# Filter loads regrouped over two queues, half of an angle table on GpSimd and a small identity made earlier, in a fused Fourier-filter and gated-MLP kernel

## The chip, the cores and the metric

The kernel runs on one core of one Trainium2 chip. The metric is the time of one execution on the device, in microseconds (us), lower is better. Before the change: 802.13 us (median of 3 runs, 801.12 to 802.29).

Names of engines in the profile: PE is TensorE's matmuls, PEld its weight loads, DVE is VectorE, ACT ScalarE, POOL GpSimd, SP SyncE. A "q" behind an engine's name is its sequencer, which issues DMA transfers.

## The reference

```python
# x: [8, 3008, 256], filt_r and filt_i: [1505, 256]
X = np.fft.rfft(x, axis=1)
y = np.fft.irfft(X * (filt_r + 1j * filt_i)[None], n=3008, axis=1)
# then, on the 24064 tokens, w_in: [256, 2048], w_out: [2048, 256], beta: [2048]
h = y.reshape(24064, 256) @ w_in
out = (h * sigmoid(beta * h)) @ w_out
```

## The kernel before

The Fourier transforms are matmuls: 3008 = 47 x 64, first a transform of length 47, then one of length 64 with the twiddle factors in its table (`t2`), then the product with the filter, then the same two steps backwards. The tables are made on the core, from angles and the sine function. Seven of the eight batches are filtered in the shadow of the MLP, whose 752 steps (`hps`, `gT`, `acc`) keep PE busy. The first batch can't hide: everything it needs must be done before the first MLP matmul. I call the time up to that matmul **the head**.

```python
KG = 6                                   # the 24 rows of the filter come in groups 0-5, 6-11, 12-23
x_cur = load_x(0, X_FIRST)               # six loads on GpSimd's queue (they cast to bf16)
bt = ...; nc.sync.dma_start(bt[:], moe_beta...)

mark = dpool.tile([1, D], BF16, name="mark", tag="mark")
nc.sync.dma_start(mark[:], x_cur[:1, JG, :])      # a tiny store: SyncE stands here until the
                                                  # third load of x has landed
...
FG = ((0, KG), (KG, KG), (2 * KG, 2 * KG))
for k0, n in FG:
    load_filter(fr_sb, filt_r, 0, k0, n, nc.sync) # real half: partitions 0-63 of fr_sb (two loads)
for k0, n in FG:
    load_filter(fr_sb, filt_i, M, k0, n, gp)      # imaginary half: partitions 64-127, GpSimd's queue
WG = NFB // 4
ws = [load_wout(i * WG, WG) for i in range(2)]    # SyncE's queue
...                                               # GpSimd: `keep`, five tiny operations
held = setup.tile([P, 1], F32, name="held", tag="held")
for p0 in (H, M + H):                             # GpSimd stands here until group 1 has landed,
    gp.tensor_copy(held[p0 : p0 + H], fr_sb[p0 : p0 + H, 2 * KG - 1, :1])
for h in range(WI):
    gp.dma_start(win_sb[:, :, fs], ...)           # then loads w_in, and later x of the second batch
# ... tables, angles(0, nc.vector), angles(1, nc.vector), first1(0..7) = first stage, 8 x 8 matmuls ...

def beta_columns():                               # in the loop below, at i == 3
    bps = hpsum.tile([P, NFB], F32, name="bps", tag="hps")
    id_f = setup.tile([NFB, NFB], F32, name="id_f", tag="id_f")
    gp.tensor_copy(id_f[:], ident[:NFB, :NFB])
    nc.tensor.transpose(bps[:], bt[:], id_f[:])
    ...

def product(i):                                   # 12 of them, for two rows each
    ...                                           # 4 matmuls into ps and ps2q
    for dst, ps in zip((p_t, q_t), pss):
        nc.vector.tensor_tensor(dst[:], ps[:], fr_sb[:, 2 * i : 2 * i + 2, :], ALU.mult)

for i in range(NK // 2 + FLAG):
    product(i); ...; t2_part(1, i); ...           # t2_part(1, .): ScalarE, needs angles(1)
    if i == 3: t2_more(1, nc.vector); beta_columns()
    ...
```

In the MLP's first steps the kernel loads both filter halves once more, in another layout (`uf`: `fi_sb` at step 1, the real half a few steps later, 3 MB), and the second batch's first-stage result goes through memory to be turned (`d<-a` writes it, `a<-d` reads it). The second batch's next stage, at step 22, needs all of these.

Of the kernel before, what the change touches and what calls it, by code (L numbers as in the profile page):

```python
# [9 lines left out]
P = 128  # L10
# [3 lines left out]
F32 = mybir.dt.float32  # L14
# [10 lines left out]
M = 64  # L25
H = M // 2
NK = 24
J = 32
KG = 6
NG = NK // KG  # L30
JG = 8
# [5 lines left out]
def kernel(  # L37
# [10 lines left out]
    nc = tc.nc  # L48

    B, S, D = x.shape  # L50
    NF = filt_r.shape[0]
    DIN, FF = moe_w_in.shape
# [4 lines left out]
    NFB = FF // P  # L57
# [8 lines left out]
    dpool = ctx.enter_context(tc.tile_pool(name="dram_scratch", bufs=2, space=bass.MemoryType.DRAM))  # L66
# [18 lines left out]
    fr_sb = consts.tile([P, NK, D], F32, name="fr_sb", tag="fr_sb")  # L85
# [8 lines left out]
    ident = consts.tile([P, P], BF16, name="ident", tag="ident")  # L94
# [3 lines left out]
    win_sb = wpool.tile([P, NDC, FF], BF16, name="win_sb", tag="win_sb")  # L98
# [4 lines left out]
    def evac(dst, src, on_act, scale=None):  # L103
        if on_act:
            nc.scalar.activation(dst, src, ACT.Copy, scale=1.0 if scale is None else scale)  # L105
        elif scale is None:
            nc.vector.tensor_copy(dst, src)  # L107
        else:
            nc.vector.tensor_scalar_mul(dst, src, scale)  # L109

    def load_x(b, parts):
        t = xpool.tile([NP, J, D], BF16, name="xg", tag="xg")
        xv = x[b].rearrange("(p j) d -> p j d", j=J)
        for p0, p1, j0, j1 in parts:
            nc.gpsimd.dma_start(t[p0:p1, j0:j1, :], xv[p0:p1, j0:j1, :])  # L115
        return t
# [7 lines left out]
    def load_filter(f_sb, filt, at, k0, n, eng, later=False):  # L124
        lo = AP(filt.tensor, filt.offset + k0 * D, [[N1 * D, H], [1, n * D]])
        hi = AP(filt.tensor, filt.offset + (N1 - k0) * D, [[N1 * D, H], [-D, n], [1, D]])
        units = [
            lambda: eng.dma_start(
                f_sb[at : at + H, k0 : k0 + n, :].rearrange("p k d -> p (k d)"), lo
            ),  # L130
            lambda: eng.dma_start(f_sb[at + H : at + M, k0 : k0 + n, :], hi),
        ]
        if later:
            return units
        for go in units:
            go()

    def load_wout(f0, n):
        ws = ostp.tile([P, n, D], F32, name="ws", tag="ost")
        nc.sync.dma_start(  # L140
            ws[:], moe_w_out[f0 * P : (f0 + n) * P, :].rearrange("(fb fp) j -> fp fb j", fp=P)
        )
        return ws

    def scale_wout(ws, f0, n, eng):
        for i in range(n):
            eng.tensor_scalar_mul(
                wout_sb[:, f0 + i, :], ws[:, i, :], rbeta_sb[:, f0 + i : f0 + i + 1]
            )
# [3 lines left out]
    setup = sp.enter_context(tc.tile_pool(name="setup", bufs=1))  # L153
# [25 lines left out]
    def warm(n, cols=512):  # L179
        for _ in range(n):  # L180
            nc.tensor.matmul(pw[0][:, :cols], lhsT=wz[:, :P], rhs=wz[:, :cols], start=True, stop=True)
# [5 lines left out]
    x_cur = load_x(0, X_FIRST)  # L187
# [1 line left out]
    nc.sync.dma_start(bt[:], moe_beta.rearrange("(fb fp) -> fb fp", fp=P))  # L189

    mark = dpool.tile([1, D], BF16, name="mark", tag="mark")
    nc.sync.dma_start(mark[:], x_cur[:1, JG, :])

    gp = nc.gpsimd
    ip_f = small("ip_f")
# [3 lines left out]


    FG = ((0, KG), (KG, KG), (2 * KG, 2 * KG))
    for k0, n in FG:
        load_filter(fr_sb, filt_r, 0, k0, n, nc.sync)
    for k0, n in FG:
        load_filter(fr_sb, filt_i, M, k0, n, gp)

    WG = NFB // 4
    ws = [load_wout(i * WG, WG) for i in range(2)]

    m_p = small("m_p")  # L210
    gp.tensor_scalar(m_p[:], ip_f[:], float(M), float(-M), ALU.is_ge, ALU.mult)
# [2 lines left out]
    gp.tensor_tensor(keep[:], keep[:], m_p[:], ALU.mult)  # L214
    gp.tensor_scalar(keep[:], keep[:], 0.5, None, ALU.is_gt)


    held = setup.tile([P, 1], F32, name="held", tag="held")
    for p0 in (H, M + H):
        gp.tensor_copy(held[p0 : p0 + H], fr_sb[p0 : p0 + H, 2 * KG - 1, :1])  # L220
    WI = 2
    for h in range(WI):
        fs = slice(h * FF // WI, (h + 1) * FF // WI)
        gp.dma_start(win_sb[:, :, fs], moe_w_in[:, fs].rearrange("(dc p) f -> p dc f", p=P))

    pre = small("pre")
    nc.scalar.activation(pre[:], wz[:, :1], ACT.Silu)
# [42 lines left out]
    def angles(h, eng):  # L270
        u = setup.tile([P, NH, M], F32, name="u", tag=f"u{h}")
        r = setup.tile([P, NH, M], F32, name="r", tag=f"r{h}")
        eng.tensor_tensor(
            u[:],
            ka[:, h * NH : (h + 1) * NH].unsqueeze(2).broadcast_to([P, NH, M]),
            kb[:].unsqueeze(1).broadcast_to([P, NH, M]),
            ALU.add,
        )
        eng.tensor_scalar(r[:], u[:], ROUND_C, ROUND_C, ALU.add, ALU.subtract)
        eng.tensor_tensor(u[:], u[:], r[:], ALU.subtract)  # L280
        us.append(u)
        rs.append(r)

    def t2_part(h, part):
        u, r = us[h], rs[h]
        ks_ = slice(h * NH, (h + 1) * NH)
        if part == 0:
            nc.scalar.activation(t2[:, ks_, 2, :], u[:], ACT.Sin, scale=TWO_PI)
        elif part == 1:
            nc.scalar.activation(r[:], u[:], ACT.Abs)  # L290
        else:
            for cols, sgn, b in ((slice(0, H), -1.0, hp), (slice(H, M), 1.0, hm)):
                nc.scalar.activation(
                    t2[:, ks_, 1, cols], r[:, :, cols], ACT.Sin, scale=sgn * TWO_PI, bias=b[:]
                )
# [5 lines left out]
        eng.tensor_copy(t2[:, ks_, 0, :], t2[:, ks_, 1, :])  # L301

    angles(0, nc.vector)
    angles(1, nc.vector)


    a_t = ypool.tile([P, NDC, NK, J, 4], BF16, name="a_t", tag="y")
# [1 line left out]
    def first1(i, on_act):  # L309
        for dc in range(NDC):  # L310
            if dc:
                ps = opsum.tile([P, 4, P], F32, name="psa", tag="acc")
            else:
                ps = fpsum.tile([P, 4, P], F32, name="psa", tag="f")
            for e in range(4):
                nc.tensor.matmul(
                    ps[:, e, :KP],
                    lhsT=x_cur[:, 4 * i + e, dc * P : (dc + 1) * P],
                    rhs=t1b[:],
                    start=True,  # L320
                    stop=True,
                )
            evac(
                a_t[:, dc, :, 4 * i : 4 * i + 4, :].rearrange("p k j a -> p j k a"),
                ps[:, :, :KP].rearrange("p j (k a) -> p j k a", a=4),
                on_act[dc],
            )
# [2 lines left out]
        first1(i, (True, True))  # L330
        warm(2)
    t2_part(0, 0)
    first1(2, (True, True))
    warm(2)
    for part in (1, 2):
        t2_part(0, part)
# [5 lines left out]
    warm(2)  # L342
    first1(6, (True, True))
    warm(2)
    first1(7, (False, True))

    xs = {}
    if B > 1:
# [42 lines left out]

    def beta_columns():
        bps = hpsum.tile([P, NFB], F32, name="bps", tag="hps")
        id_f = setup.tile([NFB, NFB], F32, name="id_f", tag="id_f")
        gp.tensor_copy(id_f[:], ident[:NFB, :NFB])
        nc.tensor.transpose(bps[:], bt[:], id_f[:])
        tiny = setup.tile([P, NFB], F32, name="tiny", tag="tiny")
        nc.vector.tensor_copy(beta_sb[:], bps[:])
        gp.tensor_tensor(tiny[:], beta_sb[:], beta_sb[:], ALU.mult)
        gp.tensor_scalar(tiny[:], tiny[:], 1e-12, 2e-6, ALU.is_lt, ALU.mult)  # L400
        gp.tensor_tensor(beta_sb[:], beta_sb[:], tiny[:], ALU.add)
        gp.tensor_copy(
            t1.rearrange("p (a k) -> p a k", a=4), t1b.rearrange("p (k a) -> p a k", a=4)
        )
# [56 lines left out]
    for i in range(NK // 2 + FLAG):  # L461
        if i < NK // 2:
            product(i)
        if i % 3 < 2 and i // 3 < 3:
            turn_a(2 + 2 * (i // 3) + i % 3, True)
        if i < 3:
            t2_part(1, i)
        if i % 3 > 0 and i // 3 < 3:
            table3(1 + i // 3, 4 - 2 * (i % 3), i % 3 == 1)
        if i == 3:  # L470
            t2_more(1, nc.vector)
            beta_columns()
        if i == 7:
            nc.vector.reciprocal(rbeta_sb[:], beta_sb[:])
        if i == 9:
            table4()
        if i >= FLAG:
            inverse3(i - FLAG)

    for i in range(4):  # L480
        if i >= 2:
            ws.append(load_wout(i * WG, WG))
        scale_wout(ws[i], i * WG, WG, gp)

# [257 lines left out]
    for s in range(len(steps) + LAG):  # L742
        if s < len(steps):
            i, fb = steps[s]
# [24 lines left out]
        if s >= LAG:  # L769
            i, fb = steps[s - LAG]  # L770
# [18 lines left out]
            if fb == NFB - 1:  # L789
                ost = ostp.tile([P, 4, D], F32, name="ost", tag="ost")  # L790
                for h in range((nch + 1) // 2):
                    n = min(2, nch - 2 * h)
# [38 lines left out]
```

## Time and profile before

| | before |
|---|---|
| time, median of 3 | 802.13 us |
| first filter product starts (DVE) | 20.79 us |
| last filter product ends | 42.52 us |
| first MLP matmul (`hps`), end of the head | 47.20 us |
| PE idle before `bps`, waiting for `id_f` | 3.21 us |
| TensorE clock at half | 10.2 us, from about 23 to 33.3 us |
| from the end of the last `d<-a` to the next-stage matmul | 71.11 to 74.51 us |

Busy time by windows. The columns are the window, then its length and, per engine, busy us and number of instructions, then the granted clock, the DMA engines' busy share and GB/s:

```profile
...
core 0: us, PE busy (x) PEld busy (x) DVE busy (x) ACT busy (x) POOL busy (x), PEclk, DMA share, GB/s
16.00:23.00 7.00, 3.57 (x48) 3.15 (x48) 2.49 (x5) 6.57 (x12) 0.00 (x0) 1.00 0.98 224
23.00:33.30 10.30, 7.09 (x56) 6.05 (x54) 5.90 (x13) 4.10 (x6) 5.30 (x13) 0.50 1.13 244
33.30:43.00 9.70, 9.22 (x127) 8.18 (x125) 9.15 (x17) 7.14 (x13) 5.79 (x7) 1.00 0.81 165
100.00:797.00 697.00, 693.62 (x5334) 488.96 (x5334) 327.19 (x508) 529.28 (x801) 100.56 (x85) 1.00 0.38 105
...
```

From 100 us on PE is busy 693.6 of 697 us: that part can't move. In the head the clock stands at 0.50 between 23.0 and 33.3 us, and the DMA engines are busy almost throughout (shares of 0.98, 1.13 and 0.81).

Timeline of DVE (start, length, engine, line, operation, tiles; in brackets the idle time before it and what ended it):

```profile
...
20.79 0.69 DVE L430 TENSOR_TENSOR pb_t<-ps,fr_sb 128x512 bf16<-128x512 f32 x1 [4.51 <-DMA fr_sb<-in_filt_r_dram]
...
28.43 0.17 DVE L398 COPY beta_sb<-bps 128x16 f32<-128x16 f32 x1 [1.49 <-PE bps L396]
29.82 0.69 DVE L430 TENSOR_TENSOR pb_t<-ps,fr_sb 128x512 bf16<-128x512 f32 x1 [1.22 <-PE ps L421]
...
32.80 0.69 DVE L430 TENSOR_TENSOR pb_t<-ps,fr_sb 128x512 bf16<-128x512 f32 x1 [1.70 <-PE ps L421]
...
41.84 0.68 DVE L430 TENSOR_TENSOR qb_t<-ps2q,fr_sb 128x512 bf16<-128x512 f32 x1
```

The first product waits 4.51 us for the filter. Later there are three more gaps, of 1.49, 1.22 and 1.70 us, each behind PE. Why PE is late stands in its own timeline and in GpSimd's:

```profile
...
22.13 0.38 PE L421 MATMUL ps2q<-a,t 128*128 128x256 bf16 x2 [3.35 <-DVE qb_t L430]
...
28.11 0.28 PE L396 MATMUL bps<-id_f,bt 16*128 16x16 f32 x1 [3.21 <-POOL id_f L395]
...
47.20 1.02 PE L753 MATMUL hps<-y,win_sb 128*128 128x512 bf16 x4
```

```profile
...
23.47 0.42 POOL L220 COPY held<-fr_sb 32x1 f32<-32x1 f32 x2 [10.76 <-DMA fr_sb<-in_filt_r_dram]
24.00 1.56 POOL L224 DMA_DIRECT2D win_sb<-in_moe_w_in_dram  x2
25.55 2.27 POOL L115 DMA_DIRECT2D xg<-in_x_dram  x4
27.86 0.19 POOL L395 CAST id_f<-ident 16x16 f32<-16x16 bf16 x1
...
```

PE waits 3.21 us for `id_f`, a 0.19 us copy. It is late only because GpSimd works in order and it stands behind `held` (which waited 10.76 us for filter group 1) and six DMA issues.

SyncE's issues, and what each queue (q0 is GpSimd's, q1 SyncE's) moved from 9.5 to 13.8 us:

```profile
...
9.43 0.27 SPq L192 DMA_DIRECT2D mark<-xg  x1
9.74 0.33 SPq L128 DMA_DIRECT2D fr_sb<-in_filt_r_dram  x1
10.11 0.42 SPq L131 DMA_DIRECT2D fr_sb<-in_filt_r_dram  x1
...
```

```profile
...
DMA packets 290, 1.02 MB, mean 238 GB/s; under 512 B 72, under 2 KB 72, under 8 KB 290
...
q0 software_dynamic: 290, 1.02, 105.4%
...
```

SyncE had issued loads from 9.43 us on, but nothing of them moved in this window: all 1.02 MB belong to GpSimd's queue.

The chain of waits from 63 us on (start, length, what):

```profile
...
63.54 7.57 DMA d<-a
...
71.18 3.29 DMA a<-d
...
74.51 0.38 PE ps L578 x2
...
```

### The profile page before, as it was taken

Reading aid. Unit: us, or ns where it says so; the run is one execution under the profiler, and the core shown is the slowest. Engines: PE = TensorE matmul, PEld = TensorE weight load, DVE = VectorE, ACT = ScalarE, POOL = GpSimd, SP = SyncE. Lnnn points to the kernel's source line nnn. Section 1 sums busy time; section 2 is a strip of 40 time slices with the busy share of each in tenths; the row PEclk is TensorE's granted clock in tenths of the full one; section 3 lists DMA queues with packets and bytes.
Section 4 is the critical chain, followed back from the end, with each engine's and each line's share of the span. In section 5 each row is a group of like instructions: output and inputs, shape, how many; then the busy total and the mean of one; then the engine's idle time right before and its main releaser. Section 6 shows DMA issues by size and latency. Waiting matters only on the chain.

```text
span 800.1 us, 15381 instructions
## 1 busy us (share of the span) xinstructions
PE 780.2 (98%) x6101; PEld 550.2 (69%) x6101; DVE 398.8 (50%) x644; ACT 599.1 (75%) x920; POOL 144.0 (18%) x150
## 2 busy tenths in 40 slices
PE   7799999999999999999999999999999999999997
PEld 4666667776677766776678766687667776776665
DVE  6774945574527655374644655347462770500100
ACT  6577887787677866788667886778767788677776
POOL 4460510240003300042001310023100340000000
PEclk9799999999999999999999999999999999999999
DMA  8978469323931167211880119502290114110101
GB/s 188 228 186 213 92 168 213 115 98 97 218 108 71 67 163 191 87 48 66 197 217 27 68 68 214 178 28 92 87 244 27 67 74 114 39 53 28 54 27 53
DMA packets 84337, 91.43 MB, mean 114 GB/s; under 512 B 3597, under 2 KB 75038, under 8 KB 83372
## 3 DMA queue, kind: packets, MB, share of 16 engines
q1 hardware_dynamic: 79930, 72.11, 30.4%
q0 software_dynamic: 2400, 14.94, 9.8%
q10 hardware_dynamic: 1936, 3.41, 2.0%
q8 instruction: 47, 0.77, 0.4%
q14 instruction: 24, 0.20, 0.1%
HBM read 57.16 MB, written 46.66 MB: 130 GB/s over the span
## 4 chain that ended last, share of the span: by engine, by line
PE 89%; DMA 4%; DVE 3%; issue 2%; ACT 1%; POOL 1%; SPq 0%; ACTq 0%; DVEq 0%; POOLq 0%
PE acc L781 39%; PE hps L753 38%; PE ps L556 3%; PE ps L504 2%; PE ps L578 2%; PE ps L605 2%; DMA fr_sb<-in_filt_r_dram 2%; DVE ost L107 1%; DMA d<-a 1%; DMA xg<-in_x_dram 1%; PE psz L440 0%; POOL xg L115 0%; DVE p_t L588 0%; DMA a<-d 0%; DVE q_t L589 0%
## 5 line engine op out<-in xcount | busy, mean ns | idle before, releaser
L762 ACT ACTIVATE gT<-hps,beta_sb 128x512 bf16<-128x512 f32 x752 | 516.7, 687 | 177.6 <-PE hps L753 168.4
L781 PE MATMUL acc<-wout_sb,gT 128*128 128x256 bf16 x3008 | 455.2, 272 | 1.5 <-DVE ost L107 0.3
L753 PE MATMUL hps<-y,win_sb 128*128 128x512 bf16 (+7 forms) x1728 | 447.7, 351 | 0.0
L781 PEld LDWEIGHTS <-gT 128*128 128x128 bf16 x3008 | 285.7, 98 | 132.5 <-issue 4.6
L753 PEld LDWEIGHTS <-win_sb 128*128 128x128 bf16 x1728 | 164.8, 98 | 24.8 <-issue 0.5
L595 POOL TENSOR_TENSOR v_t<-p_t,q_t 128x512 bf16<-128x512 f32 x84 | 106.7, 1270 | 378.0 <-DVE q_t L592 370.5
L107 DVE COPY ost<-acc 128x512 f32<-128x512 f32 x87 | 56.2, 684 | 195.7 <-PE acc L781 188.4
L107 DVE CAST a<-ps 96x512 bf16<-96x512 f32 x96 | 65.9, 686 | 83.5 <-PE ps L556 82.6
L109 DVE TENSOR_SCALAR y<-ps 128x376 bf16<-128x376 f32 x118 | 64.5, 548 | 61.5 <-PE ps L504 61.4
L588 DVE TENSOR_TENSOR p_t<-ps,fr_sb 128x512 f32<-128x512 f32 x84 | 58.1, 692 | 33.6 <-PE ps L578 32.2
L592 DVE TENSOR_TENSOR q_t<-ps,fi_sb 64x512 f32<-64x512 f32 x84 | 58.3, 694 | 1.2
L589 DVE SCALAR_TENSOR_TENSOR q_t<-ps,fi_sb 64x512 f32<-64x512 f32 x84 | 57.4, 684 | 1.1
L504 PEld LDWEIGHTS <-zz 96*128 96x128 bf16 x512 | 35.4, 98 | 29.7 <-DVE q_t L592 0.8
L105 ACT ACTIVATE z<-ps 128x512 bf16<-128x512 f32 x84 | 49.6, 590 | 0.8 <-PE ps L556 0.5
L556 PE MATMUL ps<-xg,t 94*96 94x512 bf16 x112 | 41.9, 381 | 0.3 <-DVE zz L107 0.2
L504 PE MATMUL ps<-t,zz 96*128 96x94 bf16 x448 | 36.8, 205 | 0.0
L578 PE MATMUL ps<-a,t 128*128 128x256 bf16 x168 | 32.1, 273 | 1.4 <-DMA a<-d 1.4
L115 POOL DMA_DIRECT2D xg<-in_x_dram x22 | 12.0, 553 | 116.4 <-PE acc L781 97.4
L605 PE MATMUL ps<-v_t,t 128*128 128x256 bf16 x168 | 32.1, 273 | 0.3 <-DVE q_t L592 0.3
L578 PEld LDWEIGHTS <-t 128*128 128x128 bf16 x168 | 15.9, 98 | 16.3 <-issue 1.6
L556 PEld LDWEIGHTS <-t 94*96 94x96 bf16 x112 | 13.8, 123 | 12.5 <-issue 0.7
L605 PEld LDWEIGHTS <-t 128*128 128x128 bf16 x168 | 15.4, 98 | 8.1 <-DVE q_t L592 0.5
(113 smaller groups left out, 207.2 us busy)
## 6 DMA issues: line engine op xcount, KB each, us to landing
out_dram<-ost SPq DMA_DIRECT2D x40, 512.0 KB, 2.9
d<-a SPq DMA_DIRECT2D x28, 384.0 KB, 11.3
a<-d SPq DMA_DIRECT2D x28, 384.0 KB, 4.5
d<-z SPq DMA_DIRECT2D x28, 384.0 KB, 3.6
zz<-d SPq DMA_DIRECT2D x28, 384.0 KB, 6.5
xg<-in_x_dram POOLq DMA_DIRECT2D x6, 1280.0 KB, 10.2
out_dram<-ost SPq DMA_DIRECT2D x20, 128.0 KB, 2.5
ws<-in_moe_w_out_dram SPq DMA_DIRECT2D x4, 512.0 KB
```

The lines of the kernel that those rows point to most:

```text
L107: nc.vector.tensor_copy(dst, src)
L109: nc.vector.tensor_scalar_mul(dst, src, scale)
L504: nc.tensor.matmul(ps[:, e, :NP], lhsT=zz[:, jj + e, dc * P : (dc + 1) * P], rhs=tab[:], start=True, stop=True,)
L556: nc.tensor.matmul(ps[:KP], lhsT=t1[:], rhs=s["x"][:, 2 * i : 2 * i + 2, :], start=True, stop=True)
L578: nc.tensor.matmul(ps[:, e, :], lhsT=t2[:, k0 + e, 3:5, :].rearrange("p c k -> p (c k)"), rhs=s["a2"][g][:, kk + e, :], start=True, stop=True,
L588: nc.vector.tensor_tensor(p_t[:], ps[:], fr_sb[:, k0 : k0 + 2, :], ALU.mult)
L592: nc.vector.tensor_tensor(q_t[:M], ps[M:P], fi_sb[M:P, k0 : k0 + 2, :], ALU.mult)
L595: nc.gpsimd.tensor_tensor(v_t[:], p_t[:], q_t[:], ALU.add)
L605: nc.tensor.matmul(ps[:, e, :], lhsT=t3[:, k0 + e, :], rhs=v_t[:, e, :], start=True, stop=True)
L753: nc.tensor.matmul(hps[:, pos - t0 : pos - t0 + ln], lhsT=win_sb[:, dc, fb * P : (fb + 1) * P], rhs=ys[b][:, dc, n0 : n0 + ln], start=(dc ...
L762: nc.scalar.activation(gT[:, :tn], hps[:, :tn], ACT.Silu, scale=beta_sb[:, fb : fb + 1])
L781: nc.tensor.matmul(acc[tb // 2][:, tb % 2, :], lhsT=gT[:, tb * P : (tb + 1) * P], rhs=wout_sb[:, fb, :], start=(fb == 0 and tb % 2 == 0), ...
```

## The change

Its intent: have the first filter group (both halves) on SyncE's queue as soon as the first part of x is there, so that the products start sooner; split the rest of the filter over both queues; take half of the angles from VectorE; let `w_out` wait until group 1 is there (`mark2`); and make `id_f` early, before GpSimd has to stand.

```diff
-    nc.sync.dma_start(mark[:], x_cur[:1, JG, :])
+    nc.sync.dma_start(mark[:], x_cur[:1, 0, :])
...
-    for k0, n in FG:
+    load_filter(fr_sb, filt_r, 0, *FG[0], nc.sync)
+    load_filter(fr_sb, filt_i, M, *FG[0], nc.sync)
+    for k0, n in FG[1:]:
         load_filter(fr_sb, filt_r, 0, k0, n, nc.sync)
-    for k0, n in FG:
         load_filter(fr_sb, filt_i, M, k0, n, gp)
-
-    WG = NFB // 4
-    ws = [load_wout(i * WG, WG) for i in range(2)]
...
-    held = ... (the two copies and the two loads of w_in: moved down, unchanged)
+    id_f = setup.tile([NFB, NFB], F32, name="id_f", tag="id_f")
+    gp.tensor_copy(id_f[:], ident[:NFB, :NFB])
...
     angles(0, nc.vector)
-    angles(1, nc.vector)
+    angles(1, gp)
+    held = ... (as before)
+    mark2 = dpool.tile([1, 2 * D], F32, name="mark2", tag="mark2")
+    for c, p0 in enumerate((M - 1, P - 1)):
+        nc.sync.dma_start(mark2[:, c * D : (c + 1) * D], fr_sb[p0 : p0 + 1, 2 * KG - 1, :])
+    WG = NFB // 4
+    ws = [load_wout(i * WG, WG) for i in range(2)]
...
-    first1(2, (True, True))          # evacuations: True = ScalarE, False = VectorE
+    first1(2, (False, False))
...
-    first1(7, (False, True))
+    first1(7, (False, False))
...
     def beta_columns():
         bps = hpsum.tile([P, NFB], F32, name="bps", tag="hps")
-        id_f = setup.tile([NFB, NFB], F32, name="id_f", tag="id_f")
-        gp.tensor_copy(id_f[:], ident[:NFB, :NFB])
```

More of the change, by code (lines that the diff above doesn't have):

```diff
@@ L215 @@
     gp.tensor_scalar(keep[:], keep[:], 0.5, None, ALU.is_gt)
-    held = setup.tile([P, 1], F32, name="held", tag="held")
-    for p0 in (H, M + H):
-        gp.tensor_copy(held[p0 : p0 + H], fr_sb[p0 : p0 + H, 2 * KG - 1, :1])
-    WI = 2
-    for h in range(WI):
-        fs = slice(h * FF // WI, (h + 1) * FF // WI)
-        gp.dma_start(win_sb[:, :, fs], moe_w_in[:, fs].rearrange("(dc p) f -> p dc f", p=P))
+    id_f = setup.tile([NFB, NFB], F32, name="id_f", tag="id_f")
+    gp.tensor_copy(id_f[:], ident[:NFB, :NFB])
     pre = small("pre")
@@ L303 @@
     angles(0, nc.vector)
-    angles(1, nc.vector)
+    angles(1, gp)
+    held = setup.tile([P, 1], F32, name="held", tag="held")
+    for p0 in (H, M + H):
+        gp.tensor_copy(held[p0 : p0 + H], fr_sb[p0 : p0 + H, 2 * KG - 1, :1])
+    WI = 2
+    for h in range(WI):
+        fs = slice(h * FF // WI, (h + 1) * FF // WI)
+        gp.dma_start(win_sb[:, :, fs], moe_w_in[:, fs].rearrange("(dc p) f -> p dc f", p=P))
+    mark2 = dpool.tile([1, 2 * D], F32, name="mark2", tag="mark2")
[3 more added lines that the diff above has]
+    ws = [load_wout(i * WG, WG) for i in range(2)]
     a_t = ypool.tile([P, NDC, NK, J, 4], BF16, name="a_t", tag="y")
```

## The prediction

> **What bounds the kernel.** The page gives PE 780.2 of 800.1 us busy; from 100 us on it is busy 693.6 of 700 (windows). The change leaves that work alone, so only the first 75 us can move. The head, up to the first hidden-layer matmul at 47.20 us (timeline), costs:
>
> - DVE (timeline): the first product waits 4.51 us for the filters and starts at 20.79; the last ends at 42.52. Between them lie 24 products 0.60 us apart, three table copies, three negate/copy passes: about 17.3 us. 4.4 us are gaps.
> - PE waits 3.2 us (24.9 to 28.1) for `id_f`, which stands on GpSimd behind the `held` copies; these wait 10.8 us for filter group 1 (waits).
> - Clock 0.50 from 23.0 to 33.3 (windows), after 3.35 us of PE idleness. The Trainium skill, "TensorE: Matmul & The Clock Gate", Part 1, says an idle window of about 3.4 us halves the clock; 10.2 us agree.
> - DMA share about 1.0 from 5 to 40 us.
>
> **What changes.**
>
> 1. `id_f` early: removes the 3.2 us PE wait and the DVE gaps after it (1.5, 1.2, 1.7 us). The half clock should end after one busy window (3.4 us) instead of three. Worth 2.5 to 3 us by itself.
> 2. Filter group 0 (0.79 MB) is issued by SyncE from 6.5 us on; its real half was issued at 9.7. I doubt the gain: from 9.5 to 13.8 us the SyncE queue had work and moved nothing, while GpSimd's moved 1.02 MB (DMA by window); from 24 to 28 it was the other way round. A later queue waits for the other's backlog. Now x and 1.18 MB of imaginary groups 1 and 2 are GpSimd's. At about 225 GB/s group 0 lands between 17 us (queues share) and 21.5 (it waits). I take 19.8, a gain of 1 us; early landing would also avoid the half clock.
> 3. Second angles: 2.5 us leave DVE (0.96+0.56+0.96). On GpSimd I estimate 6 us, from `v_t` 1.27 us for 512 columns and `wout` scaling 0.92 for 256; done at about 16.5, needed by ACT at 18.5. Nothing on the chain.
> 4. Evacuations moved to DVE: 0.3 us, hidden.
> 5. `w_out` waits for group 1 (`mark2`), needed only from about 29 us.
>
> The last product ends near 38 us; the main loop starts 4.3 (1.8 to 8) us earlier.
>
> **What is given back.** Filter reload, second batch's load and its scratch round trip follow at once. The chain of waits shows 7.57 us (`d<-a`) and 3.29 us (`a<-d`) before 74.5 us, PE idle 1.36 us. DMA is idle only about 5 us between 41 and 51. This wait grows to about 1.5 to 2.5 us: a large gain is capped near 5.5 us, a small one keeps nearly all.
>
> Net gain about 4 us: **798.0 us**, 8 in 10 between 794.8 and 800.8. Faster by over 2%: 0.01; within 2%: 0.98; slower: 0.01.
>
> **What would show it.** Right: no PE wait for `id_f`; half clock at most 3.5 us, or none; first product between 17 and 21 us, last near 38; first hidden-layer matmul near 43; the `a<-d` wait, near 70, about 2 us; then a constant shift. Wrong: ACT waiting for GpSimd's `u`.
>
> **What would make it wrong.** Group 0 crowding x, so that first-stage matmuls wait for x beyond 12.8 us; GpSimd's angles over 8 us; another phase of the clock's window; late `w_out` loads pushing the reload far behind.

## The result

After: 799.86 us (median of 4, 798.22 to 800.22); before, of the same rounds: 801.62 us (median of 4, 800.9 to 802.29). The ratio is 0.9974, 95% interval 0.9957 to 0.9992, so about 2.1 us less. (Ratios here are the mean time of one kernel's fast runs over that of the other's of the same rounds, so not quite the ratio of the medians that are quoted.) By a threshold of 2% that is "same"; the interval says it is a little faster.

| | before | after |
|---|---|---|
| first filter product starts | 20.79 us | 21.58 us |
| last filter product ends | 42.52 us | 38.47 us |
| first MLP matmul | 47.20 us | 43.14 us |
| PE's wait for `id_f` | 3.21 us | none |
| half clock in the head | 10.2 us | none |
| next-stage matmul after `a<-d` | 74.51 us | 70.99 us |
| span of the profiled execution | 800.1 us | 797.6 us |

The windows of after, to be held against those of before:

```profile
...
16.00:23.00 7.00, 3.81 (x52) 3.31 (x51) 2.33 (x5) 6.29 (x12) 0.46 (x1) 1.00 1.08 218
23.00:33.30 10.30, 8.99 (x127) 8.25 (x127) 10.30 (x22) 7.63 (x13) 4.99 (x12) 1.00 1.06 230
33.30:43.00 9.70, 8.46 (x107) 6.66 (x105) 6.86 (x12) 6.39 (x13) 7.25 (x8) 1.00 1.05 229
...
```

The clock is 1.00 throughout, and DVE is busy for all of 23 to 33.3 us (5.90 us before).

DVE, PE and GpSimd:

```profile
...
21.14 0.35 DVE L395 TENSOR_SCALAR fr_sb<-fr_sb,keep 64x256 f32<-64x256 f32 x1 [4.21 <-DMA fr_sb<-in_filt_i_dram]
21.58 0.69 DVE L434 TENSOR_TENSOR pb_t<-ps,fr_sb 128x512 bf16<-128x512 f32 x1
...
27.71 0.16 DVE L402 COPY beta_sb<-bps 128x16 f32<-128x16 f32 x1
...
37.79 0.68 DVE L434 TENSOR_TENSOR qb_t<-ps2q,fr_sb 128x512 bf16<-128x512 f32 x1
...
```

```profile
...
22.93 0.38 PE L425 MATMUL ps2q<-a,t 128*128 128x256 bf16 x2 [3.11 <-DVE qb_t L434]
...
43.14 1.02 PE L757 MATMUL hps<-y,win_sb 128*128 128x512 bf16 x4
...
```

```profile
...
10.04 0.19 POOL L216 CAST id_f<-ident 16x16 f32<-16x16 bf16 x1
10.21 1.46 POOL L265 TENSOR_TENSOR u<-ka,kb 128x768 f32<-128x768 f32 x1
11.76 2.81 POOL L271 TENSOR_SCALAR r<-u 128x768 f32<-128x768 f32 x1
14.65 1.81 POOL L272 TENSOR_TENSOR u<-u,r 128x768 f32<-128x768 f32 x1
23.11 0.42 POOL L301 COPY held<-fr_sb 32x1 f32<-32x1 f32 x2 [6.65 <-DMA fr_sb<-in_filt_r_dram]
...
```

The products now follow each other without a gap, but they start no sooner: they start 0.79 us later. The last part of group 0 lands at 21.01 us, in before it landed at 20.67. The real half was issued 3.5 us sooner (6.25 us against 9.74), but the imaginary half, which before's GpSimd issued at 5.56 and 6.12 us, is now issued later, at 7.08 and 7.86 us (SyncE's issues, then the chain):

```profile
...
5.94 0.27 SPq L192 DMA_DIRECT2D mark<-xg  x1
6.25 0.33 SPq L128 DMA_DIRECT2D fr_sb<-in_filt_r_dram  x1
6.62 0.42 SPq L131 DMA_DIRECT2D fr_sb<-in_filt_r_dram  x1
7.08 0.74 SPq L128 DMA_DIRECT2D fr_sb<-in_filt_i_dram  x1
7.86 0.44 SPq L131 DMA_DIRECT2D fr_sb<-in_filt_i_dram  x1
...
```

```profile
...
1.36 4.56 DMA xg<-in_x_dram
...
7.86 13.14 DMA fr_sb<-in_filt_i_dram
...
21.14 0.36 DVE fr_sb L395
...
```

The last of the four loads of group 0 is issued at 7.86 us and takes 13.14 us. The angles on GpSimd took 1.46 + 2.81 + 1.81 = 6.1 us and ended at 16.46 us; ScalarE first read them at 19.58 us. Nobody waited for them.

And the later wait of the chain:

```profile
...
59.64 7.86 DMA d<-a
...
67.59 3.36 DMA a<-d
...
70.99 0.38 PE ps L582 x2
...
```

To see what becomes of the 4.06 us won in the head, I held the start times of all 752 MLP activations of the two profiles against each other. The lead is 4.06 us at step 0, 3.52 us after the read of step 22, and 2.36 us from step 84 on, where PE waits 1.20 us for the third batch's `a<-d`. At the last step it is 2.43 us. So half of what the head won is gone at the end of this pair of profiles. The experiments show which part of that is the change's and which part is chance.

### The profile page after: what moved, and what is told of

Its sections match the earlier page's. It is cut to its first block, busy times and chain, and to the rows that moved or that the text cites. A ratio compares the mean times of both kernels' runs of the same rounds, so it can differ in the third digit from the quotient of the medians.

```text
span 797.6 us, 15291 instructions
## 1 busy us (share of the span) xinstructions
PE 771.2 (97%) x6005; PEld 547.4 (69%) x6101; DVE 397.6 (50%) x644; ACT 597.2 (75%) x917; POOL 150.4 (19%) x151
## 3 DMA queue, kind: packets, MB, share of 16 engines
q10 hardware_dynamic: 1936, 3.41, 2.1%
## 4 chain that ended last, share of the span: by engine, by line
PE 86%; DMA 7%; DVE 3%; issue 2%; ACT 1%; SPq 0%; POOL 0%; DVEq 0%; ACTq 0%; POOLq 0%
PE acc L785 39%; PE hps L757 35%; DMA d<-a 4%; PE ps L560 3%; PE ps L508 3%; PE ps L582 2%; PE ps L609 2%; DMA fr_sb<-in_filt_i_dram 2%; DVE ost L107 1%; DMA a<-d 1%; DMA xg<-in_x_dram 1%; PE psz L444 0%; DVE p_t L592 0%; ACT a L105 0%; ACT gT L766 0%
## 5 line engine op out<-in xcount | busy, mean ns | idle before, releaser
L757 PE MATMUL hps<-y,win_sb 128*128 128x512 bf16 (+7 forms) x1634 | 427.4, 350 | 0.1
L560 PEld LDWEIGHTS <-t 94*96 94x96 bf16 x112 | 13.8, 123 | 12.6 <-issue 0.9
```

The lines of the kernel that those rows point to most:

```text
L560: nc.tensor.matmul(ps[:KP], lhsT=t1[:], rhs=s["x"][:, 2 * i : 2 * i + 2, :], start=True, stop=True)
L757: nc.tensor.matmul(hps[:, pos - t0 : pos - t0 + ln], lhsT=win_sb[:, dc, fb * P : (fb + 1) * P], rhs=ys[b][:, dc, n0 : n0 + ln], start=(dc ...
```

## The experiments

Two remarks. All landings of single loads below, and those in the expectations, are taken from the semaphore updates in the trace; the expectations count them from a zero that lies 0.24 us before the profile's, the text and tables here use the profile's. And where a median in us is quoted, the runs of before beside it, on the same chip, are given too, because chips differ.

Summary of the head, one profile each ("late" and "early" is `id_f`; "old" is before's order of filter loads, "split" that of the change, "one queue" is e3 and e9):

| kernel | id_f | loads | first product | last product ends | first MLP matmul | half clock in the head |
|---|---|---|---|---|---|---|
| before | late | old | 20.79 | 42.52 | 47.20 | 10.2 |
| before_again | late | old | 19.15 | 39.31 | 43.99 | 3.4 |
| e1_idf_only | early | old | 21.35 | 38.18 | 42.86 | 3.4 |
| e1_again | early | old | 19.20 | 36.03 | 40.70 | 0 |
| e1_third | early | old | 19.41 | 36.27 | 40.95 | 0 |
| e2_idf_late | late | split | 21.15 | 41.27 | 45.94 | 10.2 |
| after | early | split | 21.58 | 38.47 | 43.14 | 0 |
| after_again | early | split | 21.46 | 38.67 | 43.35 | 3.4 |
| e4_angles_dve | early | split | 22.03 | 39.08 | 43.76 | 6.8 |
| e5_x3_later | early | split | 21.39 | 38.44 | 43.12 | 3.4 |
| e6_no_reload | early | split | 21.39 | 38.28 | 42.96 | 3.4 |
| e12_idf_split | early | split | 21.46 | 38.29 | 42.97 | 0 |
| e3_one_queue | early | one queue | 18.55 | 36.61 | 41.29 | 0 |
| e9_one_queue_ws | early | one queue | 18.85 | 36.83 | 41.51 | 3.4 |

### e1_idf_only, e1_again, e1_third: the identity alone

Before, with nothing but this:

```diff
     gp.tensor_scalar(keep[:], keep[:], 0.5, None, ALU.is_gt)
+    id_f = setup.tile([NFB, NFB], F32, name="id_f", tag="id_f")
+    gp.tensor_copy(id_f[:], ident[:NFB, :NFB])
...
     def beta_columns():
-        id_f = ...
-        gp.tensor_copy(id_f[:], ident[:NFB, :NFB])
```

> Before, with nothing but the identity for beta made early. Theory A (the gain in the head is the removal of the 3.2 us wait of PE for id_f and of the half clock that it prolongs; the filter loads gave nothing): the wait is gone, the first product still starts near 20.8 us, the last product ends between 38 and 40 us, the first hidden-layer matmul starts at 42.5 to 44.5 us, total about 2 us under before, equal to after within 0.7 us. Rival B (the new loads and the angles on GpSimd carry part of the gain): first hidden-layer matmul at 45 us or later, total within 0.7 us of before.

> e1_idf_only once more, on one chip with after_again. First hidden-layer matmul at 43 +- 0.8 us. Theory C: 1.5 to 2 us under after_again. Theory D: within 1 us of it.

> e1_idf_only a third time, beside e12 and e9 on one chip. First product 19 to 21.5 us, first hidden-layer matmul 40.5 to 43 us, total 3.5 to 5 us under before.

Measured: 796.23 us beside 801.13 of before (ratio 0.9956, interval 0.9937 to 0.9974); then 796.23 beside 801.55 (0.9935, 0.9917 to 0.9952); then 797.58 beside 802.16 (0.9946, 0.9931 to 0.9962). The mean of the three is 0.9946: 4.3 us less than before, about twice what the whole change brings. Against after_again, on the same chip and in the same rounds, the means are 796.34 and 799.60 us: **the whole change is 3.3 us slower there than its one line.** (By the ratios to before, over all sessions, it is 2.3 us.) Theory A had expected them equal, so it holds for the cause of the gain and fails for the rest of the change, which isn't neutral but costs time.

PE no longer waits for `id_f` (e1_again):

```profile
...
22.98 0.21 PE L397 MATMUL bps<-id_f,bt 16*128 16x16 f32 x1 [0.51 <-issue]
...
40.70 1.02 PE L754 MATMUL hps<-y,win_sb 128*128 128x512 bf16 x4
...
```

The expectation of the head in e1_again (43 us) was missed by more than 2 us: 40.70. In that profile, and in e1_third, the filter came sooner than in e1_idf_only. The old order has two modes, seen in `mark`: SyncE issues it when the third load of x has landed, which was at 9.43 us in before and 9.73 in e1_idf_only, but at 7.46 to 7.79 us in before_again, e1_again and e1_third. The first product follows: 20.79 and 21.35 us against 19.15, 19.20 and 19.41.

### before_again: the kernel before once more

> The kernel before once more, profiled, for the spread of what the profiles are compared by. First product between 19 and 21.5 us, PE's wait for id_f 3 us or more after the first products, a half clock of 6.8 to 10.2 us in the head, first hidden-layer matmul at 46 to 47.5 us.

```profile
...
25.68 0.23 PE L396 MATMUL bps<-id_f,bt 16*128 16x16 f32 x1 [3.26 <-POOL id_f L395]
...
43.99 1.02 PE L753 MATMUL hps<-y,win_sb 128*128 128x512 bf16 x4
...
```

The wait for `id_f` is there again, 3.26 us, and the first product starts in the expected range. But the half clock lasted one stretch of 3.4 us instead of three, and the head ends at 43.99 instead of 47.20 us, outside of what I had expected. The one profile that the prediction was worked out from was thus a slow specimen of before, by 3.2 us in the head. So the 4.06 us between the first two profiles is not the change's gain in the head: the two profiles of before end their heads at 45.6 us in the mean, those of after and after_again at 43.25, which is 2.35 us less, close to the 2.1 us of the times.

### e2_idf_late: all of the change but the identity

```diff
-    id_f = ...   (early)
     def beta_columns():
+        id_f = setup.tile([NFB, NFB], F32, name="id_f", tag="id_f")
+        gp.tensor_copy(id_f[:], ident[:NFB, :NFB])
```

> After, with the identity made late again, behind held, w_in and x of the second batch on GpSimd. Theory A: GpSimd is free for it at about 27.4 us, so PE waits about 1.3 us for it (26.2 to 27.6) and the head loses 1 to 1.5 us, not 3.2; first hidden-layer matmul near 44.3; if the half clock also comes back it is 2 to 3 us more. Rival B: head within 0.3 us of after.

Measured: 802.09 us beside 801.13 of before; ratio 1.0019, interval 1.0005 to 1.0033, so about 1.5 us **slower** than before. PE's wait for `id_f` was 1.00 us, and the half clock came back for its full 10.2 us, with the first MLP matmul at 45.94 us, just under what the expectation gives for that case (43.14 us and 3 to 4.5 us more). The two parts add up roughly: the identity alone -4.3 us, the rest alone +1.5, in sum -2.8; the whole change has -2.1 and, in after_again, -2.0 us.

The half clock is not only in the profiles. The mean granted clock of each execution is recorded. Before has 0.997 or more in 4 of its 33 executions of the three sessions (mean 0.9947), e2 in none of 5; all kernels with the identity early together have it in 42 of 62 (mean 0.9972), e1 in 15 of 18, e4 and e5 in only 2 of 5 and 2 of 6.

### e12_idf_split: the identity and the new order of the loads

e1 with the new `mark` and the new filter loop, `w_out` right behind them as in before:

```diff
-    nc.sync.dma_start(mark[:], x_cur[:1, JG, :])
+    nc.sync.dma_start(mark[:], x_cur[:1, 0, :])
...  (the filter loop of the change)
```

> e1 with one thing more of the change: the new split of the filter loads (group 0 on SyncE behind the first part of x, then the real half of groups 1 and 2 there, their imaginary half on GpSimd). Theory E (loads land in the order in which they are issued, whatever the queue, so group 0 lands behind 1.18 MB of groups 1 and 2 and later than before): last part of group 0 at 21 to 21.8 us, first product 21.3 to 22, total 0.5 to 2.5 us over e1_third. Rival F (the split is harmless and what costs the change its time against e1 is the gate on w_out, the angles or the evacuations): total within 0.4 us of e1_third.

Measured: 798.13 us beside 797.58 for e1_third (means 798.25 and 797.47, so 0.8 us more, with intervals of the ratios that overlap: 0.9941 to 0.9965 and 0.9931 to 0.9962). In time this is at the lower edge of theory E and not clear of F. In the profile it is clear: the first product starts at 21.46 us, as E expected, against 19.41 in e1_third. Over all profiles the seven with the split start it at 21.15 to 22.03 us (mean 21.5), the five with the old order at 19.15 to 21.35 (mean 20.0). The split costs 1.5 us there, in the mean.

What it does to the loads can be read from when each load of after was issued and when it landed:

| load of after | queue | issued | landed |
|---|---|---|---|
| imaginary, group 1, low | GpSimd | 5.62 | 14.37 |
| imaginary, group 1, high | GpSimd | 6.19 | 15.52 |
| **real, group 0, low** | SyncE | 6.25 | 13.08 |
| **real, group 0, high** | SyncE | 6.62 | 17.43 |
| imaginary, group 2, low | GpSimd | 6.79 | 17.89 |
| **imaginary, group 0, low** | SyncE | 7.08 | 19.33 |
| imaginary, group 2, high | GpSimd | 7.28 | 20.68 |
| **imaginary, group 0, high** | SyncE | 7.86 | 21.01 |
| real, group 1, low | SyncE | 8.35 | 21.94 |

But for the third row they land in the order in which they were issued, whatever the queue. Group 0 is on a queue of its own, but GpSimd issues 1.18 MB of groups 1 and 2 in the same 1.7 us, and group 0's last part comes behind nearly all of it. The order is what came out, not yet a cause. The bytes and packets of each queue in after say more: from 6.25 to 9.5 us GpSimd's queue moved alone (168 packets, 0.64 MB); from 10 to 18 us both moved, with nearly equal numbers of packets, 307 of GpSimd's and 302 of SyncE's, but 1.32 MB against 0.56, because GpSimd's packets are larger. So the urgent load had under a third of the bytes in these 8 us. In before, group 0's imaginary half was the first load behind x on GpSimd's queue, and only its real half was late.

### e3_one_queue: all filter loads on SyncE, group by group

```diff
     for k0, n in FG[1:]:
         load_filter(fr_sb, filt_r, 0, k0, n, nc.sync)
-        load_filter(fr_sb, filt_i, M, k0, n, gp)
+        load_filter(fr_sb, filt_i, M, k0, n, nc.sync)
```

> After, with the imaginary half of groups 1 and 2 on SyncE too, so that only x stands ahead of group 0 (all twelve filter loads on one queue, group by group). Theory (a load waits for whatever the other queue was given before it, and the 1.18 MB of groups 1 and 2 on GpSimd's queue is what keeps group 0 until 21.25 us): group 0 lands at 16.5 to 18 us, the first product starts at 17.5 to 18.5 right behind its matmuls, the last group lands near 27; last product 35.5 to 37; first hidden-layer matmul 40 to 41.5. The wait for the scratch read near 68 us then takes back part: total 1 to 2.5 us under after. Rival (SyncE's queue is slow by itself for rows of 1 KB): group 0 lands after 20 us, head as in after.

Group 0 landed at 16.22 us, 4.8 us sooner than in after, by taking nothing away but the loads of groups 1 and 2 from the other queue. The first product started at 18.55 us, now waiting 0.42 us for PE and not for the filter; the last filter load landed at 27.5 us and the head ended at 41.29 us, all within 0.1 us of what the theory expected, but for the last load ("near 27"); the rival (a slow queue) is out. The time was expected wrongly: 797.57 us beside 801.13 (ratio 0.9970, 0.9953 to 0.9987), only 0.3 us under after by the ratios. The head's lead over before, 5.9 us, shrank to 2.4 us at step 12. The waits of that stretch show it (engine, tile, line, what it waited for: us, times, longest). DVE waits for a scratch write, and PE for DVE:

```profile
...
DVE a L107 <- DMA d<-a: 2.9, 1, 2.9
...
PE ps L560 <- DVE a L107: 2.4, 1, 2.4
...
```

The second load of `w_out` landed at 42.92 us (before: 29.95), SyncE stood until 47.3 us to issue the last one, and the scratch writes behind that came late.

### e9_one_queue_ws: e3 without the gate on w_out

```diff
         load_filter(fr_sb, filt_i, M, k0, n, nc.sync)
+    WG = NFB // 4
+    ws = [load_wout(i * WG, WG) for i in range(2)]
...
-    mark2 = ...   (and the two loads of w_out behind it)
```

> e3 (all filter loads on SyncE, group by group) without the gate on w_out: its first two loads stand right behind the filters, as in before. In e3 the head won 5.9 us and lost 3.5 at the twelfth step, because w_out landed at 43.2 us, SyncE stood until 47.5 us and the scratch writes behind it came late. Theory: w_out lands near 29 and 31 us, that wait of PE (2.4 us) is gone, first hidden-layer matmul at 41 to 41.8; but the bytes in front of the scratch read are the same, so the read ends at 69 to 70.5 us: total as e1_third within 1 us. Rival (the head's gain is kept in full): 1.5 us or more under e1_third.

The main expectation failed: the two loads landed at 37.0 and 43.1 us, not near 29 and 31, and PE's wait (2.5 us) stayed. They had been issued at 16.6 and 17.5 us, before GpSimd issued `w_in` and x at 19.4 us and later, and still landed last. The queues from 28 to 40 us:

```profile
...
q0 software_dynamic: 612, 2.16, 89.2%
q1 hardware_dynamic: 616, 0.61, 18.4%
...
```

Here both queues had work and GpSimd's moved 3.5 times the bytes. So "in the order of issue" isn't the rule: it fails here. What the two cases have in common stands in the first number of each line: 612 and 616 packets, equal as in after from 10 to 18 us (307 and 302). That is what comes out when two queues take turns packet by packet; GpSimd's packets held 3.5 kB in the mean, SyncE's 1.0. It isn't so in every window (in before, 14 to 18 us: 99 and 219), no run varied the packet sizes, and why SyncE's queue moved nothing in its first 3 to 4 us behind GpSimd's stays open. The total, 798.56 us, is 1.3 us over e1_third (means 798.74 and 797.47): the expected "within 1 us" narrowly missed, and neither e3 nor e9 beats the one line.

### e4_angles_dve: the angles on VectorE again

```diff
-    angles(1, gp)
+    angles(1, nc.vector)
```

> After, with the second half of the angles on VectorE again. Theory (VectorE waits 4.2 us for group 0, so 2.5 us of angles there cost nothing): first product at 21.6 +- 0.3 us, first hidden-layer matmul at 43.1 +- 0.4, total within 0.5 us of after. Rival (the angles delay the first-stage evacuations and with them the products): first hidden-layer matmul 1 us or more later.

798.26 us, ratio 0.9978 (0.9964 to 0.9992) beside after's 0.9974. DVE still waited 3.29 us for group 0. The first product and the head end came 0.1 and 0.3 us outside the expected bands, with the filter landing 0.45 us later than in after. So moving the angles changes nothing here, as long as the filter is what DVE waits for.

### after_again: the change once more

> The change as it is, once more, beside e1_again on one chip. The first profile of it lost 0.5 us at the scratch read near 70 us and 1.2 us more at the scratch read of the third batch near 140 us, of the 4.06 us that the head had won. Theory C (the losses belong to the change: it starts its loads later or earlier, so that the read finds the queue full each time): both losses again, total 1.5 to 2 us over e1_again. Theory D (they are chance: how fast a 2.5 MB load goes varies from run to run): another pattern of losses, total within 1 us of e1_again.

799.20 us beside 801.55 (ratio 0.9975, 0.9952 to 0.9998). The losses were not there: its lead over the first profile of before is 3.84 us at step 0 and 3.79 at the end, the wait for `a<-d` at 70 us is 1.1 us (1.74 in the first profile), and at 140 us PE stands only 0.2 us. The 1.2 us at 140 us were chance, in this theory D is right. But the total is 3 us over e1_again and not within 1, in this it is wrong; theory C's number, 1.5 to 2 us, was exceeded, and not by the losses that it named: the first product came later (21.46 against 19.20 us), and with it the end of the head (43.35 against 40.70).

### e5_x3_later: a failed experiment

```diff
-            place(a - 8, a - 8, ux(b + 1), per=9)
+            at = a + 2 if b == 2 else a - 8
+            place(at, at, ux(b + 1), per=9)
```

> After, with the load of the fourth batch (x index 3) issued ten steps later, so that the last scratch write of the third batch is not queued behind its 2.5 MB. Theory (that write waits 12.8 us only because the load was given to the queues 2 us before it): write to landing under 5 us, no wait of PE at the scratch read near 140 us, total 0.5 to 1.3 us under after_again. Rival (the write is slow for other reasons): still over 10 us.

The edit didn't do what it was meant to: the load was issued at 122.02 us as before, because moving it ten steps down in the program doesn't hold GpSimd back; it has nothing to do in those steps and only waits for the x buffer. The scratch write took 11.65 us again (124.20 to 135.85), and the time, 800.12 us, is after's. It tests nothing, and after_again had hardly a wait there (0.2 us). That the write is slow because of the x load before it stays argued.

### e6_no_reload: without the second load of the real half (wrong result)

```diff
-        units += load_filter(fr_sb, filt_r, M, 0, NK, nc.scalar, True)
```

> After, without the second load of the real filter half (1.5 MB; WRONG RESULT on purpose, the numbers from the second batch on are wrong). Theory (the scratch round trip that ends near 71 us is bound by the DMA bytes queued before it, of which these are a part): the last scratch write lands 4 to 6 us earlier, near 62 instead of 67.7 us, and PE no longer waits for the read (1.9 us in the first profile of the change): first 1.5 to 2 us kept. Rival (the wait is latency of the round trip): the read ends within 1 us of after's.

PE is busy for all 15 us of the stretch in which it stood in after (e6 first, then after; columns as in the first table of windows):

```profile
...
60.00:75.00 15.00, 15.00 (x128) 10.82 (x127) 8.47 (x14) 10.94 (x18) 2.54 (x2) 1.00 0.51 166
...
```

```profile
...
60.00:75.00 15.00, 13.15 (x109) 9.46 (x110) 6.01 (x10) 9.89 (x16) 1.27 (x1) 1.00 0.84 231
...
```

The last scratch write landed at 62.27 us instead of 67.50, and the reads were issued 5.2 us sooner. 795.79 us beside 799.20 for after_again: 3.4 us less, of which 1.1 to 1.7 us is the wait in the profiles. The starts of the MLP activations place a little more: e6's lead over after_again is 0.4 us at step 0, 0.9 at step 12, 2.2 after the read and 2.3 at the end; the last 1.1 us I can't place. So the wait near 70 us is for DMA bytes in line, as the prediction had it. In no profile with the reload was the read issued before 64.8 us (e1_again); in e3 and e9, with the shortest heads among the variants of the change, it was issued at 66.4 and 66.3 us, in after at 67.6, in e6 at 62.4.

## Why the prediction was right or wrong

The time was inside the predicted range (799.86 us in 794.8 to 800.8, point 798.0), and "within 2%" was right. The gain was half of the predicted 4 us. That the total stayed inside the range was partly luck: step 1 brought about 1.5 us more than predicted, and the rest of the change cost about 2 us where step 2 predicted a gain of 1, so two misses partly cancelled. Step by step:

1. **"`id_f` early ... worth 2.5 to 3 us by itself."** Right in mechanism, too small: e1 brings 4.3 us. It takes away the 3.2 us wait, and most of the half clock: 10.2, 10.2 and 3.4 us in the three profiles with the identity late, none or one stretch of 3.4 us in ten of the eleven with it early (two in e4, 6.8 us; e1_idf_only's, and one of e4's, began at 11 to 12 us, before any product). The products, from first to last, take 20.1 to 21.7 us with the identity late (three profiles) and 16.8 to 17.2 us with it early and the loads split or old (nine profiles).
2. **"Group 0 lands between 17 us and 21.5. I take 19.8, a gain of 1 us."** This is the term that was mis-sized, and its sign was wrong. The doubt was right (a later queue waits for the other's backlog, shown by e12's landings and by e3), the number taken was not: it landed at 21.01 us, and the first product starts 1.5 us later than with the old order, in the means. I took a middle between waiting and an even share. What came was first waiting (from 6.25 to 9.5 us GpSimd's queue moved alone, as the window from 9.5 to 13.8 us of before had shown) and then an uneven share: 0.56 of 1.88 MB from 10 to 18 us. The imaginary half, which was first in line behind x in before and landed at 14.25 us there, had moreover been moved back.
3. **Second angles: "nothing on the chain", "6 us".** Right: 6.1 us, and e4 shows no difference.
4. **Evacuations: hidden.** Nothing speaks against it; not tested alone.
5. **The main loop 4.3 us earlier.** The profiles' difference, 4.06 us, seemed to confirm it. It compared a slow specimen of before with after. In the means of two profiles each it is 2.35 us.
6. **"Given back": the wait for `a<-d` grows to about 2 us, then a constant shift.** The wait was 1.74 and 1.1 us (1.36 before). That it is DMA bytes in line is shown by e6. The shift was constant in after_again; in the first profile 1.2 us more were lost at 140 us, by chance.

What stays open: after_again and after have ratios of 0.9974 and 0.9975, e12 has 0.9953. Between them lie the gate on `w_out`, the angles and the evacuations. The angles are cleared by e4. The profiles of e12 and after_again hardly differ (first MLP matmul 42.97 and 43.35 us; lead over before at the last step 3.72 and 3.79 us). The runs were on different chips, and e1's own ratio differs as much between chips (0.9935 to 0.9956), so the difference may be none. I have no run that separates the gate from the rest.

The best version found is e1, the kernel before with the identity made early and nothing else: 796.23 us beside 801.55 of before and 799.20 of the change on the same chip.

## What to carry to other kernels

A tiny operation on an engine that works in order can be the costliest line of a stage, if it stands behind something that waits: look first at what the waiting operation needs, and make it before the queue jams. Putting an urgent load on its own queue didn't put it ahead here: count the bytes that any queue has been given before it, look at the packet sizes on both queues, and hold back the loads that aren't urgent. And when a change is worth a few us, take two or three profiles of the kernel before: here one profile of it was 3 us off the next, as much as the change.

## What the Trainium skill lacked or had wrong

- "DMA: Bandwidth & Descriptors", section "Queues, rings and completion order", says that each DMA engine round-robins between the queue rows it has work for, at packet granularity. The runs agree where both queues moved: 307 packets of GpSimd's queue against 302 of SyncE's in after from 10 to 18 us, 612 against 616 in e9 from 28 to 40 us (packets as the profile counts them), though the bytes were 1.32 MB against 0.56 and 2.16 against 0.61. What it lacks is the start: from 9.5 to 13.8 us of before SyncE's queue had work and moved nothing, while GpSimd's moved 1.02 MB. Its section "Issuing engines are not separate DMA queues", by which a second issuing engine saves only the time of issuing, fits: group 0 on a queue of its own came no sooner (first product at 21.5 us in the mean, 20.0 with the old order).
- "GPSIMD Engine Reference", section 4.1, says that operations with one input are roughly at line rate and those with two about 2x slower than on VectorE. Two inputs agree roughly: 1.46 and 1.81 us for 128x768 fp32 against 0.96, 1.5 and 1.9 times (times on GpSimd are rough in this profile). The one-input `tensor_scalar` with two operations (add, subtract) took 2.81 us on GpSimd and 0.56 on VectorE, five times as long.
- "TensorE: Matmul & The Clock Gate", Part 1, agrees: the half clock came in stretches of 3.41 us or three of them (10.24), the page has windows of 3413 ns. It calls the slow start of a kernel run-variable; these runs add how much the head of one kernel differed: 10.2 us of half clock in one profile of before, 3.4 in the next, and an end of the head 3.2 us apart, though part of that is the filter's landing.
